# A fused attention, MoE and MLP kernel: landing times in the attention planner, four one-hot tiles on ScalarE, the experts' order chain in PSUM

## The chip, the cores and the metric

One core of a Trainium2 chip runs the whole program in one launch. The metric is the device time of that launch in microseconds, the median of several runs. The profile is one more execution of the same program, taken by the hardware profiler.

## The reference, cut to what matters

```
x = attention(q, k, v, omega)     # 4 x 8 heads x 576 x 64, random features, 128 of them
x = x.reshape(2304, 512)
logits = x @ w_gate               # 8 experts
e = argmax(logits); gate = softmax(logits)[e]
x[mask_e] = gate * (relu(x[mask_e] @ w1[e]) @ w2[e])     # 512 -> 1024 -> 512
h = x @ w_in                      # 512 -> 2048
g = where(h >= 1, h, where(h <= -1, 0, (h + 1)**2 / 4))
out = g @ w_out                   # 2048 -> 512
```

Attention here is linear: `phi(x) = exp(x @ omega.T - |x|^2 / 2 - max)`, then `phi(q) @ (phi(k).T @ v)`, divided by `phi(q) @ sum(phi(k))`.

## The kernel before, in words

Three stages follow each other: attention with routing, the experts, and the last MLP.

**Attention.** The 2304 tokens are 18 tiles of 128. Keys and queries are loaded in blocks and worked on in 36 units of half a block. A unit is: four transposes on TensorE (L646), a copy to SBUF on ScalarE (`th`, L651), 16 projections onto omega, each issued for both halves (L658), the row maximum on VectorE (L663), the bias (L670), and eight exponentials on ScalarE in two sets of four (`pp`, L674). The squares of a block are taken on ScalarE for keys (`sqt`, L600) and on GpSimd for queries, and are summed on GpSimd and VectorE into `nsq`. Key units end in the products with v (L699) and a copy `kvz` (L703); query units in transposes, a product with `kvz` and a copy `nx` (L774) for each tile.

**Routing** works on two tiles at a time (`r_tasks`): argmax, counts, and for each tile a one-hot row over 384 places, `ob` (L918, `one_b`), from which TensorE builds the list of tokens of each expert (`place`, L926). For the last pair of tiles this ends in `gidx` (L935), the list of the first expert's tokens. The last two tiles also scale their rows (L878 on ScalarE, L881 on VectorE) and store them to `xd` (L889, L892).

**What sets the order.** The attention stage is not issued in the order of the code. Every step is handed to `Plan.add` with an engine, a cost in ns, a rank, the steps that it follows and the buffers that it takes. A table of numbers, `NUDGES`, shifts the ranks. `Plan.run` then plays the stage with these costs and writes the instructions out in the order of the starts that it found. On the chip each engine runs its own list in that order and waits on semaphores. Costs are therefore no times: they only decide the order.

**The order chain** (L1080 to L1122) is some 40 small VectorE instructions between attention and the experts. It sorts the experts by their number of tokens, and moves the lists accordingly. It reads the counts `pn`, which lie in a PSUM tile of the attention's ring (`ps0`).

**The start of the experts** (`m_x0`, from L1202). GpSimd gathers the first expert's tokens from `xd` in three pieces (L1177). TensorE in the meantime runs 14 warm-up multiplications of ones (L1209) into a PSUM tile `idle`, then transposes the first piece (L1183), 3 more warm-ups, the second piece, 3 more, and the third. ScalarE splits the result (`xh`, L1189), and the first real multiplication is L1230:

```
idle = ps_h.tile([P, 512], F32, name="ph", tag="ph").rearrange("p (a f) -> p a f", a=4)
for i, _ in rows(0):
    for _ in range((14, 3, 3)[i]):
        nc.tensor.matmul(idle, lhsT=oneb, rhs=oneb.rearrange("p (o f) -> p o f", o=1).to_broadcast([P, 4, P]),
                         start=True, stop=True)
    for d in range(4):
        m_turn(0, d, i, px[d])
```

The pool of `idle` (`ps_h`) is opened after that of the attention's ring (`psp`) is closed, in the same eight PSUM banks; a tile of it is written only when the tile that lay there has been read for the last time.

Of the kernel before, what the change touches and what calls it, by code (L numbers as in the profile page):

```python
# [19 lines left out]
P = 128  # L20
# [65 lines left out]
class Plan:  # L86
# [7 lines left out]
    SLACK = 10.0  # L94
    HOPS = {"PE": {"PE": 30.0, "ACT": 200.0, "DVE": 200.0, "POOL": 200.0, "SP": 200.0},
# [26 lines left out]
    def run(self):  # L122
# [8 lines left out]
        at = {t[0]: 0.0 for t in self.tasks}  # L131
# [80 lines left out]
def kernel(  # L212
# [268 lines left out]
    with ExitStack() as actx:  # L481
# [59 lines left out]
        def omega_tasks():  # L541
# [12 lines left out]
            def scaled():  # L554
                nc.scalar.activation(oms, at(pb)[:, 0, :], AF.Copy, scale=SCALE)

            def tri():
                nc.vector.tensor_copy(trib, cs[:, C_TRI:C_TRI + P])

            x = add("SP", 1300, load_cs, 0)  # L560
            add("DVE", 130, tri, 8, after=[x])
            x = add("SP", 100, load, -7.5)
            x = add("PE", 110, turn, -5, after=[x], take=[pb], mode="whole")
            return add("ACT", 240, scaled, -5, after=[x], use=[pb])

        wgr = ac.tile([P, 4, E], F32, name="wgr")
# [509 lines left out]
        def flat(t):  # L1076
            return t[:, :, 0]
# [679 lines left out]
```

## Time and profile before

| | |
|---|---|
| three runs | 775.65, 777.16, 778.07 us; median 777.16 |
| the profiled execution | 776.65 us, of which its span is 774.9 |
| TensorE busy | 745.1 us, 96% of the span |
| VectorE, ScalarE, GpSimd busy | 515.7, 436.7, 376.6 us |
| mean granted TensorE clock | 0.991 of full speed |

Busy time is the time in which an engine had an instruction in flight, so a TensorE at 96% is not one at its peak; what an engine waits for is read from the stage concerned. Times in the rows below are microseconds from the start of the span, unless marked ns.

### The profile page before, as it was taken

What the parts mean: (1) busy time and instruction counts of PE and PEld (TensorE: products, weight loads), DVE (VectorE), ACT (ScalarE), POOL (GpSimd) and SP (SyncE); (2) the same over time, 40 slices, a digit from 0 to 9 for tenths busy, and PEclk for the clock granted to TensorE, in tenths of its full rate; (3) what the DMA queues carried; (4) which work ended last, traced back from release to release, by engine and by line L of the source; (5) the groups of instructions that cost most, each with busy time, mean ns of one, the idle gap of its engine ahead of it and who ended that gap; (6) DMA issues with size and microseconds to landing.
All of it is one profiled execution on the core that took longest, in us unless ns stands there. A gap on an engine that the chain in (4) does not pass through costs nothing. (4 is left out here: it accounts for less than half of the span.)

```text
span 774.9 us, 17116 instructions
## 1 busy us (share of the span) xinstructions
PE 745.1 (96%) x6476; PEld 684.0 (88%) x6476; DVE 515.7 (67%) x1104; ACT 436.7 (56%) x1061; POOL 376.6 (49%) x429
## 2 busy tenths in 40 slices
PE   5799999699999999999999999899999999999997
PEld 4698899489999999999988889788998899889985
DVE  3688888965667567565686775876656766575553
ACT  5999999353322222222477766676577655763441
POOL 6665951645654564425548875323343143343212
PEclk9999999899999999999999999999999999999999
DMA  9949511356765765655537769798696996977822
GB/s 231 230 100 255 158 69 30 123 166 179 213 193 178 221 212 179 207 166 161 163 117 305 274 249 330 285 328 269 177 375 189 307 319 168 332 239 285 315 97 85
DMA packets 94236, 164.25 MB, mean 212 GB/s; under 512 B 28528, under 2 KB 61424, under 8 KB 94144
## 3 DMA queue, kind: packets, MB, share of 16 engines
q1 hardware_dynamic: 79680, 94.96, 39.2%
q0 software_dynamic: 14112, 67.44, 27.0%
q8 instruction: 53, 0.87, 0.4%
q10 hardware_dynamic: 352, 0.66, 0.3%
q14 instruction: 39, 0.32, 0.1%
HBM read 122.93 MB, written 40.11 MB: 210 GB/s over the span
## 5 line engine op out<-in xcount | busy, mean ns | idle before, releaser
L1433 PE MATMUL po<-wh,g 128*128 128x512 f32 x288 | 113.8, 395 | 0.7 <-ACT st L1439 0.7
L1435 PE MATMUL po<-wh,g 128*128 128x512 f32 x288 | 113.9, 395 | 0.0
L1434 PE MATMUL po<-wl,g 128*128 128x512 f32 x288 | 113.6, 395 | 0.0
L351 POOL TENSOR_TENSOR wl<-wz,wh 128x256 fp32r<-128x256 f32 (+1 forms) x43 | 40.5, 948 | 95.3 <-ACT wh L365 92.8
L674 ACT ACTIVATE pp<-ps,bi 128x128 f32<-128x128 f32 x288 | 84.4, 487 | 0.0
L329 POOL TENSOR_SCALAR wh<-wra 128x1024 fp32r<-128x1024 f32 x43 | 50.2, 1170 | 61.2 <-DMA wra<-in_moe_w_dram 26.9
L1248 PE MATMUL py<-hh,wh 128*128 128x288 f32 (+6 forms) x256 | 77.5, 303 | 0.0
L1230 PE MATMUL ph<-xh,wh 128*128 128x288 f32 (+6 forms) x256 | 76.7, 300 | 0.7 <-ACT xh L1189 0.4
L1231 PE MATMUL ph<-xl,wh 128*128 128x288 f32 (+6 forms) x256 | 76.6, 299 | 0.1
L1250 PE MATMUL py<-hh,wl 128*128 128x288 f32 (+6 forms) x256 | 76.6, 299 | 0.0
L1232 PE MATMUL ph<-xh,wl 128*128 128x288 f32 (+6 forms) x256 | 76.5, 299 | 0.0
L1249 PE MATMUL py<-hl,wh 128*128 128x288 f32 (+6 forms) x256 | 76.3, 298 | 0.0
L1395 DVE TENSOR_TENSOR g<-cl,g 128x384 fp32r<-128x384 f32 x78 | 47.0, 603 | 38.9 <-ACT g L1391 37.9
L1235 ACT ACTIVATE hh<-ph 128x288 fp32r<-128x288 f32 (+6 forms) x64 | 26.7, 418 | 70.2 <-PE ph L1232 69.1
L1435 PEld LDWEIGHTS po<-wh,g 128*128 128x128 f32 x288 | 54.2, 188 | 13.1 <-DVE g L1395 0.4
L1433 PEld LDWEIGHTS po<-wh,g 128*128 128x128 f32 x288 | 54.2, 188 | 12.4 <-ACT st L1439 1.0
L1434 PEld LDWEIGHTS po<-wl,g 128*128 128x128 f32 x288 | 54.2, 188 | 11.5
L1236 DVE SCALAR_TENSOR_TENSOR hl<-ph,hh 128x288 fp32r<-128x288 f32 (+6 forms) x64 | 29.3, 461 | 52.0 <-ACT hh L1235 51.7
L1391 ACT ACTIVATE g<-cl 128x384 fp32r<-128x384 f32 x78 | 40.5, 520 | 39.7 <-DVE cl L1390 38.4
L441 DVE TENSOR_TENSOR wl<-wra,wh 128x1024 fp32r<-128x1024 f32 x43 | 61.0, 1421 | 2.4 <-POOL wh L329 2.4
L1253 ACT ACTIVATE yT<-py 128x288 f32<-128x288 f32 (+7 forms) x32 | 13.4, 418 | 83.6 <-PE py L1250 80.5
L663 DVE TENSOR_REDUCE nsq<-ps 128x4 f32<-128x512 f32 x72 | 48.1, 683 | 8.1 <-PE ps L658 8.0
(226 smaller groups left out, 2149.8 us busy)
## 6 DMA issues: line engine op xcount, KB each, us to landing
yS<-yd POOLq DMA_DIRECT2D x32, 768.0 KB, 12.2
wra<-in_moe_w_dram SPq DMA_DIRECT2D x43, 512.0 KB, 4.1
ys<-yd POOLq DMA_DIRECT2D x25, 768.0 KB, 11.9
wraw<-in_moe_w_dram SPq DMA_DIRECT2D x20, 512.0 KB, 4.0
yd<-tt SPq DMA_DIRECT2D x24, 384.0 KB, 2.7
yd<-ys SPq DMA_DIRECT2D x9, 768.0 KB, 4.3
wra<-in_moe_w_in_dram SPq DMA_DIRECT2D x12, 512.0 KB, 5.4
wra<-in_moe_w_out_dram SPq DMA_DIRECT2D x11, 512.0 KB, 7.6
```

Of the source, the lines that this page charges most:

```text
L329: nc.gpsimd.tensor_scalar(out=hi, in0=t, scalar1=1.0, scalar2=1.0, op0=ALU.mult, op1=ALU.mult)
L441: nc.vector.tensor_sub(lo, t, hi.bitcast(F32))
L674: act.activation(at(ppb)[:, 2 * j + i, :], at(pjb[i])[:, j, :], AF.Exp, bias=r["bi"][:, j, i:i + 1])
L1230: nc.tensor.matmul(ph, lhsT=wh[:, d, c], rhs=xh, start=(d == 0), stop=False)
L1231: nc.tensor.matmul(ph, lhsT=wh[:, d, c], rhs=xl, start=False, stop=False)
L1232: nc.tensor.matmul(ph, lhsT=wl[:, d, c], rhs=xh, start=False, stop=(d == 3))
L1248: nc.tensor.matmul(py, lhsT=wh[:, a, c], rhs=hh, start=(f == 0), stop=False)
L1249: nc.tensor.matmul(py, lhsT=wh[:, a, c], rhs=hl, start=False, stop=False)
L1250: nc.tensor.matmul(py, lhsT=wl[:, a, c], rhs=hh, start=False, stop=(f == 7))
L1433: nc.tensor.matmul(po, lhsT=gh[:, c], rhs=wh, start=(f == 0), stop=False)
L1434: nc.tensor.matmul(po, lhsT=gh[:, c], rhs=wl, start=False, stop=False)
L1435: nc.tensor.matmul(po, lhsT=gl[:, c], rhs=wh, start=False, stop=(f == 3))
```

## The change

Three things, in one diff.

1. The planner: the loads' costs are changed (a block 2250 to 1900 ns, a v 6500 to 6000, a weight 1460 to 1900, and others), the loading queue starts at 1150 ns instead of 0 (`FIRST`), and the table `NUDGES` of 1,058 numbers is another one.
2. Four tiles' one-hot rows (`OBA`, tiles 12, 13, 14 and 16) are made on ScalarE, in two instructions for each: the square of place number minus own place (`away`), and relu(1 - square). VectorE makes the negated places for them (`nr`).
3. The order chain keeps `key`, `at_`, `hot` and `offe` in the PSUM tile `ps0`, where the counts lie, and copies of two of them in SBUF, so that most of its two-input instructions read one input from PSUM and one from SBUF.

```
@@ -38,... @@ NUDGES
-    2, -4, -40, -16, 43, -44, 37, -6, 17, -2, -26, 9, -18, 36, -44, -2, -29, -37, 32, -32, -8, -18, 33, 26, -23,
+    -15, -7, -43, -28, -21, -43, -16, -42, 35, -34, -15, -42, 3, 5, -16, -22, 37, 25, -34, -44, -10, -35, 16, -44,
...
     SLACK = 10.0
+
+    FIRST = {"SP": 1150.0}
...
-        at = {t[0]: 0.0 for t in self.tasks}
+        at = {t[0]: self.FIRST.get(t[0], 0.0) for t in self.tasks}
...
-            x = add("SP", 1300, load_cs, 0)
+            x = add("SP", 900, load_cs, 0)
...
-            x = add("SP", 100, load, -7.5)
+            x = add("SP", 500, load, -7.5)
...
-            o["load"] = add("SP", 1800 if small else 2250, load, rank - 8, take=[o["buf"]])
+            o["load"] = add("SP", 1900, load, rank - 8, take=[o["buf"]])
...
             def mine2():
+                if any(t0 + j in OBA for j in range(n)):
+                    r["nr"] = ap.tile([P, n], F32, name="nr", tag="nr", bufs=3)
+                    dve.reduce_sum(r["nr"], r["pr"], axis=AX, negate=True)
                 dve.reduce_sum(rk, r["pr"], axis=AX)
...
                 r["ob", j] = ap.tile([P, NB * P], BF16, name="ob", tag="ob", bufs=4)
+                if t0 + j in OBA:
+                    away = ap.tile([P, NB * P], F32, name="away", tag="away", bufs=1)
+                    act.activation(away, cs[:, C_IOTA:C_IOTA + NB * P], AF.Square, bias=r["nr"][:, j:j + 1])
+                    act.activation(r["ob", j], away, AF.Relu, scale=-1.0, bias=1.0)
+                    return
...
-                ws.append(add("DVE", 430, lambda j=j: one_b(j), rank + 0.4, after=[x, places[-1]], use=[pb]))
+                ws.append(add(*(("ACT", 880) if t0 + j in OBA else ("DVE", 475)), lambda j=j: one_b(j), rank + 0.4,
+                              after=[x, places[-1]], use=[pb]))
...
+        OBA = (12,13,14,16)
...
-        n, key, at_, nums, off, offe = [small(f"t{i}", [P, E, 1]) for i in range(6)]
+        pn = plan.tiles["ps"][0]
+        sums, key, at_ = [pn[:, 0, 16 * i:16 * i + E] for i in range(3)]
+        hot = pn[:, 1, 0:E * E].rearrange("p (a b) -> p a b", a=E)
+        nums, off, n, keys = [small(f"t{i}", [P, E, 1]) for i in range(4)]
+        offe = pn[:, 3, 0:E].rearrange("p (e o) -> p e o", o=1)
...
-        pn = plan.tiles["ps"][0][:, 0, :]
-        nc.tensor.matmul(pn[:, 0:E], lhsT=oneb, rhs=rsb[:, NTILE, :], start=True, stop=True)
-        dve.memset(ones, 1.0)
-        dve.tensor_copy(flat(n), pn[:, 0:E])
-        dve.scalar_tensor_tensor(out=flat(key), in0=flat(n), scalar=8.0, in1=col(C_C8, E), op0=ALU.mult, op1=ALU.add)
-        dve.memset(key[:, 0, :], 0.0)
-        dve.tensor_tensor(out=prod[:, 0], in0=row(key), in1=key.to_broadcast([P, E, E]), op=ALU.is_lt)
+        nc.tensor.matmul(sums, lhsT=oneb, rhs=rsb[:, NTILE, :], start=True, stop=True)
+        dve.scalar_tensor_tensor(out=key, in0=sums, scalar=8.0, in1=col(C_C8, E), op0=ALU.mult, op1=ALU.add)
+        dve.tensor_scalar(out=key[:, 0:1], in0=key[:, 0:1], scalar1=0.0, scalar2=None, op0=ALU.mult)
+        dve.tensor_copy(flat(keys), key)
+        dve.tensor_copy(flat(n), sums)
+        dve.tensor_tensor(out=prod[:, 0], in0=line(key), in1=keys.to_broadcast([P, E, E]), op=ALU.is_lt)
...
         dve.reduce_sum(flat(offe), prod[:, 0], axis=AX)
...
         nc.vector.tensor_tensor(out=rr, in0=ohall, in1=offe.rearrange("p e o -> p o e").to_broadcast([P, NTILE, E]), op=ALU.mult)
```

In the changed kernel all lines after the new ones are numbered higher, by 2 in the units, by 10 in the routing's end, and by 19 from the order chain's end on: L646 is now L648, L658 is L660, L674 is L676, L1183 is L1202, L1209 is L1228, L1230 is L1249.

**Where the order moves: the start of attention, on TensorE.** The rows are the first of TensorE's list; of the projections of a unit the first stands for all 16. Before:

```order
L646 MATMUL ps_134<-ident,blk_142 128x128 x4
L552 MATMUL ps_135<-ident,om_205 128x128
L646 MATMUL ps_136<-ident,blk_143 128x128 x4
L658 MATMUL ps_137<-oms,th_151 64x128
...
L658 MATMUL ps_139<-oms,th_152 64x128
...
L646 MATMUL ps_141<-ident,blk_144 128x128 x4
```

Now:

```order
L648 MATMUL ps_134<-ident,blk_142 128x128 x4
L554 MATMUL ps_135<-ident,om_205 128x128
L660 MATMUL ps_136<-oms,th_151 64x128
...
L648 MATMUL ps_138<-ident,blk_143 128x128 x4
L648 MATMUL ps_139<-ident,blk_144 128x128 x4
L660 MATMUL ps_140<-oms,th_152 64x128
```

The first unit's projections (`th_151`) stood behind the transposes of the second block (`blk_143`) and directly ahead of the second unit's (`th_152`), with the third block's transposes (`blk_144`) behind both; now they come first, and both blocks' transposes stand together ahead of the second unit's projections.

**The end of attention, on ScalarE.** The rows follow the last copy of a tile's result (`nx`); `rex` are the softmax's exponentials, `blk` with 128x64 the scaled rows of a last tile. Before:

```order
L861 ACTIVATE rex<-ps_138 128x16
L858 ACTIVATE rex,rga<-lall,rmx 128x8 x2
L878 ACTIVATE blk_142<-nx_174,dall 128x64 x4
L889 DMA xd<-blk_148 64x512
L1189 ACTIVATE xh<-px 128x288 x2
```

Now:

```order
L863 ACTIVATE rex<-ps_136 128x16
L925 ACTIVATE away<-cs,nr 128x384
L926 ACTIVATE ob<-away 128x384
L925 ACTIVATE away<-cs,nr 128x384
L926 ACTIVATE ob<-away 128x384
L860 ACTIVATE rex,rga<-lall,rmx 128x8 x2
L880 ACTIVATE blk_143<-nx_171,dall 128x64 x4
L925 ACTIVATE away<-cs,nr 128x384
L926 ACTIVATE ob<-away 128x384
L891 DMA xd<-blk_146 64x512
L925 ACTIVATE away<-cs,nr 128x384
L926 ACTIVATE ob<-away 128x384
```

Two pairs of `away` and `ob` (tiles 12 and 13) now stand between the exponentials of the tiles before and those of the last two, a third pair behind the scaled rows, and the fourth behind the store that ScalarE issues.

**The order chain, on VectorE.** The rows begin at `gidx`, the first expert's list; `ps_134` is the tile `ps0`, in which the counts lie, `hot`, `t` and `trr` are the chain's own tiles. Before:

```order
L935 TENSOR_TENSOR gidx<-slots,ps_136 128x3
L936 TENSOR_TENSOR slots<-slots,ps_136 128x24
L1081 MEMSET u_3063 128x8
L1082 COPY t_3056<-ps_134 128x8
L1083 SCALAR_TENSOR_TENSOR t_3057<-t_3056,cs 128x8
...
L1103 TENSOR_TENSOR prod<-hot,t_3060 128x64
L1104 TENSOR_REDUCE t_3061<-prod 128x8
...
L1115 TENSOR_TENSOR trr<-seen,t_3061 128x144
L1116 TENSOR_REDUCE tsp<-trr 128x18
```

Now:

```order
L945 TENSOR_TENSOR gidx<-slots,ps_139 128x3
L946 TENSOR_TENSOR slots<-slots,ps_139 128x24
L1099 SCALAR_TENSOR_TENSOR ps_134<-ps_134,cs 128x8
L1100 TENSOR_SCALAR ps_134<-ps_134 128x1
L1101 COPY t_3073<-ps_134 128x8
...
L1121 TENSOR_TENSOR prod<-ps_134,t_3071 128x64
L1123 TENSOR_REDUCE ps_134<-prod 128x8
...
L1134 TENSOR_TENSOR trr<-seen,ps_134 128x144
L1135 TENSOR_REDUCE tsp<-trr 128x18
```

The last instruction that reads `ps_134` was the copy at L1082, the second of the chain; it is now the product `trr` at L1134, near its end.

## Rows read from the trace of the kernel before

**Rows 1.** The page, part 1: each engine's busy time, share and instructions.
```profile
PE 745.1 (96%) x6476; PEld 684.0 (88%) x6476; DVE 515.7 (67%) x1104; ACT 436.7 (56%) x1061; POOL 376.6 (49%) x429
```

**Rows 2.** Windows by stage: length, busy us of five engines, granted clock, DMA.
```profile
5.40:15.00 9.60, 8.01 (x96) 6.77 (x97) 3.33 (x10) 5.04 (x8) 6.19 (x7) 1.00 1.10 290
...
15.00:38.00 23.00, 18.08 (x412) 15.09 (x404) 16.16 (x46) 21.82 (x75) 15.83 (x16) 0.93 1.08 225
...
38.00:138.00 100.00, 99.11 (x2222) 89.18 (x2219) 84.68 (x325) 98.09 (x322) 60.04 (x78) 1.00 0.47 121
...
142.80:151.00 8.20, 2.19 (x41) 1.57 (x40) 7.63 (x41) 1.83 (x10) 4.83 (x10) 0.77 0.46 160
...
170.00:774.90 604.90, 595.30 (x3487) 553.32 (x3485) 386.67 (x603) 298.36 (x624) 273.39 (x280) 1.00 0.69 229
```

**Rows 3.** ScalarE's timeline at the start: start, us, line, tiles, idle before.
```profile
7.20 0.27 ACT L555 ACTIVATE oms<-ps 128x128 f32<-128x128 f32 x1
...
8.12 0.63 ACT L600 ACTIVATE sqt<-blk 128x512 f32<-128x512 f32 x1 [0.65 <-DMA blk<-in_k_dram]
...
9.78 1.05 ACT L600 ACTIVATE sqt<-blk 128x1024 f32<-128x1024 f32 x1
...
13.95 1.16 ACT L651 ACTIVATE th<-ps 128x512 f32<-128x512 f32 x2 [3.13 <-PE ps L646]
...
15.01 3.19 ACT L674 ACTIVATE pp<-ps,bi 128x128 f32<-128x128 f32 x12
```

**Rows 4.** TensorE's and VectorE's timelines at the start.
```profile
9.18 3.69 PE L658 MATMUL ps<-oms,th 64*64 64x128 f32 x64
...
12.80 1.68 PE L646 MATMUL ps<-ident,blk 128*128 128x128 f32 x8
...
11.22 0.69 DVE L663 TENSOR_REDUCE nsq<-ps 128x4 f32<-128x512 f32 x1 [1.88 <-PE ps L658]
```

**Rows 5.** ScalarE's waits from 5 to 38.3 us: in total, times, longest.
```profile
ACT kvz L703 <- PE ps L699: 1.2, 1, 1.2
```

**Rows 6.** VectorE's timeline at the end of attention and in the order chain.
```profile
142.85 0.18 DVE L781 TENSOR_REDUCE dall<-nx 128x8 f32<-128x16 f32 x1
...
149.27 1.02 DVE L918 TENSOR_TENSOR ob<-cs,ps 128x384 bf16<-128x384 f32 x2
...
150.81 0.16 DVE L935 TENSOR_TENSOR gidx<-slots,ps 128x3 uint32<-128x3 f32 x1 [0.43 <-PE ps L1080]
...
151.11 0.15 DVE L1082 COPY t<-ps 128x8 f32<-128x8 f32 x1
...
156.41 0.30 DVE L1115 TENSOR_TENSOR trr<-seen,t 128x144 f32<-128x144 bf16 x1
```

**Rows 7.** ScalarE's timeline at the end of attention.
```profile
142.40 0.41 ACT L774 ACTIVATE nx<-ps 128x292 f32<-128x292 f32 x1 [0.70 <-PE ps L771]
...
144.42 0.30 ACT L858 ACTIVATE rex<-lall,rmx 128x8 f32<-128x8 f32 x1 [1.53 <-DVE rmx L836]
...
146.75 0.82 ACT L878 ACTIVATE blk<-nx,dall 128x64 f32<-128x64 f32 x3 [1.65 <-issue]
```

**Rows 8.** Groups of ScalarE's instructions by line, from 385 us on.
```profile
L1383 ACT ACTIVATE cl<-cl 128x384 f32<-128x384 f32 x77 | 40.5, 526 | 2.4
```

**Rows 9.** TensorE's timeline and its waits at the experts' start.
```profile
151.32 4.50 PE L1209 MATMUL ph<-oneb 128*128 128x512 bf16 x14 [0.53 <-DVE t L1082]
...
155.69 0.41 PE L1183 MATMUL px<-ident,xg 128*128 128x128 f32 x2
...
159.13 0.40 PE L1230 MATMUL ph<-xh,wh 128*128 128x288 f32 x1 [0.44 <-ACT xh L1189]
...
PEld px L1183 <- DMA xg<-xd,gidx: 0.6, 1, 0.6
```

**Rows 10.** Windows in the warm-up multiplications (after the busy times the granted clock).
```profile
153.50:154.00 0.50, 0.50 (x3) 0.22 (x2) 0.47 (x5) 0.00 (x0) 0.50 (x1) 0.50 0.44 82
...
154.00:154.50 0.50, 0.50 (x4) 0.20 (x3) 0.50 (x6) 0.00 (x0) 0.38 (x1) 1.00 0.65 180
```

More of the change, by code (lines that the diff above doesn't have):

```diff
@@ L1016 @@
             if s == 1:
-                vload[0] = add("SP", 6500, lambda: load_v(0), s - 1)
+                vload[0] = add("SP", 6000, lambda: load_v(0), s - 1)
                 x = add("SP", 50, gate_weights, s)
@@ L1020 @@
             if s == 5:
-                vload[1] = add("SP", 6500, lambda: load_v(1), s - 5)
+                vload[1] = add("SP", 6000, lambda: load_v(1), s - 5)
             done[u] = unit_tasks(u, blocks[which, blk], s, prev)
@@ L1028 @@
                 if hf == 1 and b + 2 < B:
-                    vload[b + 2] = add("SP", 6500, lambda b=b: load_v(b + 2), s + 3, after=[last_head])
+                    vload[b + 2] = add("SP", 6000, lambda b=b: load_v(b + 2), s + 3, after=[last_head])
             new = []
@@ L1045 @@
                 wb = buf("wra")
-                x = add("SP", 1460, lambda key=key, wb=wb: w_load(key, at(wb)), s - 2, take=[wb])
+                x = add("SP", 1900, lambda key=key, wb=wb: w_load(key, at(wb)), s - 2, take=[wb])
                 x = add("POOL", 1050, lambda key=key: w_split(key), s + 1, after=[x], use=[wb])
@@ L1052 @@
                 wb = buf("wra")
-                add("SP", 1460, lambda key=key, wb=wb: w_load(key, at(wb)), s - 2, take=[wb])
+                add("SP", 1900, lambda key=key, wb=wb: w_load(key, at(wb)), s - 2, take=[wb])
         assert wk == 6
@@ L1065, in col @@
             return cs[:, c:c + n]
-        n, key, at_, nums, off, offe = [small(f"t{i}", [P, E, 1]) for i in range(6)]
+        pn = plan.tiles["ps"][0]
[3 more added lines that the diff above has]
+        offe = pn[:, 3, 0:E].rearrange("p (e o) -> p e o", o=1)
         inc, ones, nv = [small(f"u{i}", [P, E]) for i in range(3)]
-        hot, prod = small("hot", [P, E, E]), small("prod", [P, NB, E, E])
+        prod = small("prod", [P, NB, E, E])
@@ L1070, with column, line @@
         g = prod[:, 0:2].rearrange("p m a b -> p (m a b)").rearrange("p (e j) -> p e j", j=16)
         tot = small("ttot", [P, 1])
-        def row(t):
-            return t.rearrange("p a o -> p o a").to_broadcast([P, E, E])
+        def column(t):
+            return t.rearrange("p (e o) -> p e o", o=1).to_broadcast([P, E, E])
+        def line(t):
+            return t.rearrange("p (o e) -> p o e", o=1).to_broadcast([P, E, E])
         def flat(t):
             return t[:, :, 0]
-        pn = plan.tiles["ps"][0][:, 0, :]
@@ L1080 @@
-        nc.tensor.matmul(pn[:, 0:E], lhsT=oneb, rhs=rsb[:, NTILE, :], start=True, stop=True)
-        dve.memset(ones, 1.0)
-        dve.tensor_copy(flat(n), pn[:, 0:E])
-        dve.scalar_tensor_tensor(out=flat(key), in0=flat(n), scalar=8.0, in1=col(C_C8, E), op0=ALU.mult, op1=ALU.add)
-        dve.memset(key[:, 0, :], 0.0)
-        dve.tensor_tensor(out=prod[:, 0], in0=row(key), in1=key.to_broadcast([P, E, E]), op=ALU.is_lt)
-        dve.reduce_sum(flat(at_), prod[:, 0], axis=AX)
-        iota = col(C_IOTA, E).rearrange("p (e o) -> p e o", o=1)
@@ L1088 @@
-        dve.tensor_tensor(out=hot, in0=iota.to_broadcast([P, E, E]), in1=row(at_), op=ALU.is_equal)
-        dve.tensor_tensor(out=prod[:, 0], in0=hot, in1=row(n), op=ALU.mult)
-        dve.tensor_tensor(out=prod[:, 1], in0=hot, in1=row(iota), op=ALU.mult)
+        nc.tensor.matmul(sums, lhsT=oneb, rhs=rsb[:, NTILE, :], start=True, stop=True)
+        dve.scalar_tensor_tensor(out=key, in0=sums, scalar=8.0, in1=col(C_C8, E), op0=ALU.mult, op1=ALU.add)
+        dve.tensor_scalar(out=key[:, 0:1], in0=key[:, 0:1], scalar1=0.0, scalar2=None, op0=ALU.mult)
@@ new lines @@
+        dve.tensor_copy(flat(keys), key)
+        dve.tensor_copy(flat(n), sums)
+        dve.tensor_tensor(out=prod[:, 0], in0=line(key), in1=keys.to_broadcast([P, E, E]), op=ALU.is_lt)
+        dve.reduce_sum(at_, prod[:, 0], axis=AX)
+        dve.tensor_tensor(out=hot, in0=column(col(C_IOTA, E)), in1=line(at_), op=ALU.is_equal)
+        dve.tensor_tensor(out=prod[:, 0], in0=hot, in1=line(flat(n)), op=ALU.mult)
+        dve.tensor_tensor(out=prod[:, 1], in0=hot, in1=line(col(C_IOTA, E)), op=ALU.mult)
@@ L1093 @@
         dve.tensor_copy(ints[:, 4, :], inc)
+        dve.memset(ones, 1.0)
         dve.tensor_tensor_scan(out=inc, data0=ones, data1=flat(nums), initial=0.0, op0=ALU.mult, op1=ALU.add)
@@ L1102 @@
         dve.tensor_copy(gidx[:, :, 1:E], slots[:, :, 1:E])
-        dve.tensor_tensor(out=prod[:, 0], in0=hot.rearrange("p r e -> p e r"), in1=row(off), op=ALU.mult)
+        dve.tensor_tensor(out=prod[:, 0], in0=hot.rearrange("p r e -> p e r"), in1=line(flat(off)),
+                          op=ALU.mult)
         dve.reduce_sum(flat(offe), prod[:, 0], axis=AX)
```

82 rows, old and new, of the table NUDGES are left out of this document.

## The prediction

> **What bounds the kernel now.** I read the page's busy shares first [rows 1], then windows by stage, since a share over the whole span says nothing about a stage. Of the span, 604.9 us lie behind 170 us, and there TensorE is busy for 595.3 [rows 2]. All three edits lie ahead of that, so what matters is when the experts' first real multiplication starts, at 159.13 us [rows 9]; from there on TensorE is the bound, has no slack worth naming, and passes every microsecond on to the end. In attention, from 38 to 138 us, ScalarE is busy for 98.09 and TensorE for 99.11 of 100 us [rows 2]. ScalarE is what I count by: its list is mostly exponentials, its work is the same in any order, and only 1.9 us of idle time are left there for a better order to find. At the start there is more: from 5.4 to 15 us ScalarE works 5.04 of 9.6 us, and from 15 to 38 us 21.82 of 23. Between attention and experts, 142.8 to 151 us, ScalarE works 1.83 of 8.2 us and VectorE 7.63: there VectorE is the bound. The last stretch, 150.97 to 159.13, is the gather, the warm-ups and the transposes [rows 6, 9].
>
> **The planner.** What the new order does at the start is followed on TensorE and ScalarE. Before, TensorE ran the projections of two units in one piece of 3.69 us from 9.18, and only then the next transposes, at 12.80; ScalarE, done with the third square (9.78 and 1.05 us), waited 3.13 us for them and began its exponentials at 15.01 [rows 3, 4]. Now the first unit's projections come alone. `th_151` stands behind the 0.27 us of `oms`, so is ready near 7.7; half of 3.69 us brings TensorE to 9.6; two blocks' transposes, 1.68 us as in the row at 12.80, to 11.3 [rows 3, 4]. ScalarE squares the second block from 8.12 to 8.75, waits for its transposes until about 10.6, copies (0.6), squares (1.05) and copies the third block, and is free at 12.8. VectorE needs two maxima of 0.69 us after 9.6 [rows 4] and the biases, so is done by 11.5. The exponentials thus begin at 12.8 rather than 15.01, with one copy of 0.6 us (half of 1.16) still to do: 1.6 us gained. Further on, the 1.18 us that ScalarE waited for the first v products [rows 5] go, since those now stand ahead of two units' projections in TensorE's list while ScalarE still has finished maxima to work on. I take back 0.3 for a bias that then waits on a late square. Sum: **-2.5 us**. Bounds: nothing, if the lead is lost again, and -5.7, if all idle time of ScalarE from 5.4 to 38 us went (4.56 and 1.18).
>
> In the middle, 38 to 138 us, I take **0**: the order is new, but no row says that it waits more or less. Bounds: -1.9, all of ScalarE's idle time there, and +2.4, two new waits like the one of 1.18 us.
>
> **The four one-hot rows.** On VectorE one costs 0.47 us, by the next instruction's start (two take 1.02 us in all [rows 6]); four of them less two reductions for `nr` and one added sum are -1.6 us of VectorE's 8.12 us between the last copy's sum (142.85) and the end of `gidx` (150.97). On ScalarE no row shows this pair. The nearest is a square in place over the same 128x384, 0.526 us [rows 8]; I take that for both instructions, 1.05 us for a tile. They don't lie in idle time for free, because ScalarE's list is in order: from the last copy of `nx` (142.81) follow the small exponentials (0.2), tiles 12 and 13 (2.1), the exponentials of the last two tiles (two of 0.30 with their sums read, 0.7, which before began at 144.42 and now find ScalarE busy), the gate and its reciprocal on VectorE (0.6), the scaled rows (0.82 for three, 1.1 for four [rows 7]), tile 14 (1.05), the store (0.4), tile 16 (1.05), then TensorE's placing and VectorE's sum (0.7: from 149.27 to 150.97 less the two one-hot rows' 1.02 [rows 6]); 0.2, 0.6 and 0.4 are estimates from the gaps between the rows. That makes 7.9 us, against 8.16 before: ScalarE takes over from VectorE as what ends last, and little is left, **-0.2 us**. Bounds: -1.9, if VectorE alone decides (four times 0.47), and +1.2, if ScalarE is held by the store and both reciprocals.
>
> **The order chain.** Its own length hardly changes: a memset becomes a dependent operation and a copy comes in, +0.15 us by steps of 0.2 as at 151.11; instructions with PSUM on one side take as long as those with SBUF alone. What changes is who waits for it. The first warm-up starts at 151.32 and was released by VectorE's copy L1082, the last reader of the counts' bank [rows 9, 6]. In the change that bank is read until the product `trr`, the old L1115, which ends at 156.71 [rows 6]. So TensorE stands still through the whole chain: from the end of `gidx` to the first warm-up it was 0.35 us, and will be 5.74 (150.97 to 156.71) + 0.15 + 0.06 = 5.95, **+5.6 us**. Behind it are queued all 14 warm-ups (4.50 us), the three groups of transposes, ScalarE's split and L1230. From the first warm-up to L1230 it was 7.81 us [rows 9]. The gathers, which took part in that (the weight load waited 0.6 us for one [rows 9]), are long landed then: **-0.3**, bounds 0 and -0.6. GpSimd, the gathers and VectorE don't wait for TensorE there, but nothing on the path waits for them either, so what they may gain is not seen.
>
> **The sum**: -2.5 + 0 - 0.2 + 5.6 - 0.3 = +2.6 us. The profiled execution took 776.65 us, 0.5 below the median of 777.16; 776.65 + 2.6 = **779.3 us**, 0.34% above the profiled execution. A difference of 0.3%, 2.3 us, is about what a measurement of this kernel can tell from no change, so the forecast is a slower kernel by just that much.
>
> **The rivals.**
>
> *The lead is lost in the middle.* The start gains 2.5 us, but in-order lists on four engines near full give it back: a block or a buffer that comes 2.5 us late for a ScalarE that is early. For it: VectorE too is busy for 84.68 of the 100 us [rows 2]. Against it: the lists hold the same work. 781.8 us, 0.20.
>
> *The clock stays low.* Up to 154 us the granted clock is 0.5, the lower of the two levels (1.2 GHz), and it rises 2.7 us after the first warm-up [rows 9, 10]; TensorE had done only small pieces since 142.8, at a mean of 0.77 [rows 2]. In the change it stands wholly still for 5 us before. If all 14 run at the lower level, the 1.7 us that they ran at the upper one take twice as long, +1.7: 781.0 us, 0.07. The Trainium skill ("TensorE: Matmul & The Clock Gate", "Part 1: The HAM clock gate") says that an idle array falls to the lower level, comes back only after sustained work, and that the number of matmuls at the lower level differs from run to run; by its 426.7 ns for one of 512 columns there, 14 would be an estimated 6.0 us instead of 4.50. The trace has the fall and the rise, in one execution, and cannot show the spread.
>
> *No change that can be measured.* The middle finds the 1.9 us as well: 777.4 us, 0.12. Here the planner's gain pays for the late warm-ups.
>
> *Faster: the warm-ups don't wait.* It hangs on one place, the PSUM tile of the warm-ups. If it lay in another bank than the counts, or were released by something earlier than `trr`, the +5.3 us fall away and 776.65 - 2.7 = 774.0 us are left. For it: a matmul's wait can name several engines, and the profile picks one. Against it: the 0.53 us of idle time before 151.32 end with the copy's end at 151.26, to 0.06 us [rows 6, 9]. It decides when TensorE starts its warm-ups less than 0.7 us after `gidx`. 0.06.
>
> **How the numbers follow.** The forecast has 0.55; its own range is 777.8 to 780.8, and 779.0, the bound of slower by 0.3% from the profiled execution, lies in it, so I give 0.30 of it to slower and 0.25 to no difference. Slower: 0.30 + 0.20 + 0.07 = 0.57. Same: 0.25 + 0.12 = 0.37. Faster: 0.06. The range has to reach the lost lead and the paid-for case: its top is the 781.8 of the one with 0.7 for the tail, 782.5; its bottom is the 777.4 of the other less another 1.4 of the start's bound, 776.0. The bounds of all terms together, 772 to 787, would need everything on one side.
>
> **What would show it.** Right: the first warm-up starts about 6 us after `gidx` ends, released by `trr`; TensorE idle ahead of it; L1249 comes 13.5 us after `gidx` instead of 8.16; the first exponentials near 13 us; the last `nx` copy 2 to 3 us before 142.4; `gidx` about 8 us behind that. Wrong: warm-ups within 1 us of `gidx`; a ScalarE in the middle with more than 4 us of waits, or an attention that ends more than 6 us earlier.

## The result, and the profile after

| | before | after |
|---|---|---|
| median, measured side by side | 776.51 us (774.76 to 778.07) | 782.84 us (780.63 to 784.38) |
| ratio, 95% interval | | 1.0066 (1.0047 to 1.0086) |
| profiled execution, its span | 776.65, 774.9 | 782.84, 781.0 |

The change made the kernel slower by 0.66%, twice the 0.34% that was forecast; the median lies 0.3 us above the top of the range, and the ratio on the profiled execution's own 776.65 us gives 781.8, which lies in it. In the two profiled executions the spans differ by 6.1 us. Five marks cut them into stages (all are starts of an instruction, in us):

| mark | before | after | the stage up to it |
|---|---|---|---|
| first exponentials, `pp` | 15.01 | 12.71 | -2.30 |
| last exponentials | 135.74 | 135.67 | 120.73 to 122.96, +2.23 |
| `gidx` | 150.81 | 150.86 | 15.07 to 15.19, +0.12 |
| first expert product, `ph` from `xh` | 159.13 | 164.45 | 8.32 to 13.59, +5.27 |
| end of the span | 774.9 | 781.0 | 615.77 to 616.55, +0.78 |

The rows come from the timelines of the changed kernel: start, duration, engine, line, tiles, and in brackets the idle time before and what ended it. They answer to [rows 3, 6, 9].

```profile
12.71 1.14 ACT L676 ACTIVATE pp<-ps,bi 128x128 f32<-128x128 f32 x4
...
14.01 2.37 DVE L577 COPY wgb<-wgr 64x32 f32<-64x32 f32 x2
...
13.76 0.74 POOL L609 TENSOR_TENSOR sqt<-sqt 128x256 f32<-128x256 f32 x1
14.44 1.91 POOL L604 TENSOR_TENSOR sqt<-blk 128x1024 f32<-128x1024 f32 x1
...
17.34 1.14 ACT L676 ACTIVATE pp<-ps,bi 128x128 f32<-128x128 f32 x4 [1.75 <-DVE bi L672]
...
135.67 1.31 ACT L676 ACTIVATE pp<-ps,bi 128x128 f32<-128x128 f32 x4
...
150.86 0.16 DVE L945 TENSOR_TENSOR gidx<-slots,ps 128x3 uint32<-128x3 f32 x1 [0.91 <-PE ps L1098]
...
156.64 0.29 DVE L1134 TENSOR_TENSOR trr<-seen,ps 128x144 f32<-128x144 bf16 x1
...
156.99 4.56 PE L1228 MATMUL ph<-oneb 128*128 128x512 bf16 x14 [6.14 <-DVE trr L1134]
...
164.45 0.40 PE L1249 MATMUL ph<-xh,wh 128*128 128x288 f32 x1 [0.36 <-ACT xh L1208]
```

The last three rows are the forecast's main term as it was put: TensorE stands still for 6.14 us, `trr` ends at 156.93, the warm-ups start 0.06 us later. The first rows hold what the forecast missed. ScalarE begins at 12.71, and 4.6 us later it waits 1.75 us for the biases `bi`, which VectorE computes. VectorE at that time makes two copies of 64x32, `wgb`, which take 2.37 us; in the kernel before the same two took 0.35, at 24.95. The two lines are the copies one by one in the changed kernel (durations in ns, shortest, median and longest, and the starts), and the pair in the kernel before:

```profile
L577 DVE COPY wgb<-wgr x2: 518/1180/1841, 14.0 to 14.5; 64x32 f32<-64x32 f32 x2
...
24.95 0.35 DVE L575 COPY wgb<-wgr 64x32 f32<-64x32 f32 x2
```

The first ends at 14.53 and the second at 16.38, each 0.03 us after an instruction of GpSimd (14.50 and 16.35).

Of the windows by stage, three follow on this wait (length, busy time of PE, PE's weight loads, DVE, ACT and POOL with counts, granted clock, DMA share, GB/s), and two answer to [rows 2].

```profile
15.00:20.00 5.00, 2.84 (x72) 2.31 (x64) 4.90 (x13) 3.25 (x12) 3.73 (x4) 0.99 1.22 269
20.00:25.00 5.00, 4.41 (x47) 3.16 (x40) 3.04 (x10) 5.00 (x16) 3.01 (x3) 0.50 0.99 227
25.00:30.00 5.00, 4.74 (x75) 3.44 (x73) 4.93 (x10) 4.15 (x15) 4.01 (x2) 0.83 1.10 227
...
38.00:138.00 100.00, 98.03 (x2204) 88.84 (x2200) 80.02 (x321) 97.49 (x323) 59.86 (x78) 1.00 0.46 119
142.80:151.00 8.20, 1.99 (x41) 1.55 (x41) 6.93 (x45) 6.34 (x18) 5.24 (x12) 0.70 0.48 160
```

From 15 to 20 us ScalarE works for 3.25 of 5 us and TensorE, which waits for it, for 2.84; from 20 to 25 TensorE's granted clock is the lower of its two levels (0.50, 1.2 GHz), and ScalarE loses another 0.85 us from 25 to 30. In the middle ScalarE is as full as before (97.49 to 98.09 of 100 us), so in this profile the lead is gone by 38 us, not lost bit by bit.

### The profile page after: what moved, and what is told of

Its sections match the earlier page's. It is cut to its first block, busy times and chain, and to the rows that moved or that the text cites. A ratio compares the mean times of both kernels' runs of the same rounds, so it can differ in the third digit from the quotient of the medians.

```text
span 781.0 us, 17138 instructions
## 1 busy us (share of the span) xinstructions
PE 745.9 (96%) x6476; PEld 684.8 (88%) x6476; DVE 515.6 (66%) x1104; ACT 440.4 (56%) x1069; POOL 379.8 (49%) x429
## 3 DMA queue, kind: packets, MB, share of 16 engines
q1 hardware_dynamic: 79680, 94.96, 38.3%
## 5 line engine op out<-in xcount | busy, mean ns | idle before, releaser
L676 ACT ACTIVATE pp<-ps,bi 128x128 f32<-128x128 f32 x288 | 85.5, 488 | 2.0 <-DVE bi L672 2.0
L1249 PE MATMUL ph<-xh,wh 128*128 128x288 f32 (+6 forms) x256 | 76.6, 299 | 0.6 <-ACT xh L1208 0.4
L1454 PEld LDWEIGHTS po<-wh,g 128*128 128x128 f32 x288 | 54.2, 188 | 13.1 <-DVE g L1414 0.4
```

Source lines behind the costliest of these rows:

```text
L676: act.activation(at(ppb)[:, 2 * j + i, :], at(pjb[i])[:, j, :], AF.Exp, bias=r["bi"][:, j, i:i + 1])
L1249: nc.tensor.matmul(ph, lhsT=wh[:, d, c], rhs=xh, start=(d == 0), stop=False)
L1454: nc.tensor.matmul(po, lhsT=gl[:, c], rhs=wh, start=False, stop=(f == 3))
```

## The experiments

The theory behind them: the chain's hold on PSUM costs the 5.3 us; the planner's lead is real, and is lost because plain copies from SBUF to SBUF on VectorE are held while GpSimd is in an instruction. The rival: the new orders themselves are slower. Twelve kernels were run; each row has the ratio to the kernel before on the same chip, and the marks of one profiled execution.

| kernel | median (range, runs), us | ratio, 95% | first exponentials | last | `gidx` | first expert product | span |
|---|---|---|---|---|---|---|---|
| old chain | 773.78 (772.75 to 778.98, 12) | 0.9957 (0.9938 to 0.9976) | 12.40 | 131.56 | 146.74 | 155.54 | 772.3 |
| chain alone | 783.67 (782.45 to 786.50, 6) | 1.0066 (1.0049 to 1.0083) | 13.34 | 137.56 | 152.62 | 167.82 | 784.6 |
| planner alone | 777.76 (776.82 to 780.10, 12) | 1.0001 (0.9988 to 1.0013) | 12.73 | 135.66 | 151.92 | 160.57 | 776.9 |
| rows alone | 776.43 (774.03 to 781.32, 12) | 0.9978 (0.9957 to 1.0000) | 12.65 | 133.97 | 148.32 | 157.69 | 775.3 |
| short hold | 777.63 (775.91 to 779.22, 12) | 0.9995 (0.9982 to 1.0008) | 13.34 | 133.40 | 148.59 | 159.16 | 776.8 |
| warm-ups in the ring | 777.85 (774.81 to 781.89, 12) | 0.9995 (0.9978 to 1.0012) | 12.65 | 139.36 | 154.56 | 163.80 | 780.0 |
| maxima | 781.30 (779.95 to 784.76, 8) | 1.0051 (1.0033 to 1.0069) | 12.63 | 132.81 | 148.01 | 162.31 | 778.9 |
| old chain, maxima | 774.94 (773.29 to 776.21, 7) | 0.9963 (0.9947 to 0.9979) | 12.51 | 133.06 | 148.25 | 157.15 | 773.1 |
| planner alone, maxima | 777.76 (776.74 to 778.95, 12) | 1.0001 (0.9989 to 1.0013) | 13.32 | 133.80 | 150.06 | 158.72 | 775.0 |
| six copies | 778.29 (776.62 to 780.85, 12) | 1.0006 (0.9988 to 1.0024) | 12.28 | 136.93 | 152.12 | 160.79 | 777.0 |
| six maxima | 774.57 (773.46 to 776.18, 12) | 0.9959 (0.9946 to 0.9973) | 12.51 | 134.33 | 149.52 | 158.10 | 773.9 |
| no copies | 773.67 (773.24 to 775.30, 7) | 0.9953 (0.9936 to 0.9970) | 12.42 | 132.66 | 147.85 | 156.39 | 771.8 |

### The order chain: four kernels

**Old chain**: the changed kernel with the third part of the change taken back.

```diff
-        pn = plan.tiles["ps"][0]
-        sums, key, at_ = [pn[:, 0, 16 * i:16 * i + E] for i in range(3)]
...
+        n, key, at_, nums, off, offe = [small(f"t{i}", [P, E, 1]) for i in range(6)]
...
```

> The changed kernel with the order chain of before put back; planner's start and the four one-hot rows stay. Theory (the chain's results in PSUM keep TensorE from its warm-ups, and nothing else of the change costs anything): the first warm-up comes within 0.5 us of gidx again, L1230 and its followers 5.3 us earlier against gidx than in the changed kernel, and the time falls from 782.8 to about 777.5, which is not to be told from before. Rival (the new orders of work are what slows, and the late warm-ups are paid back before the experts begin): the warm-ups come early, but the time stays near 782.

**Chain alone**: the kernel before with that part and nothing else.

> The kernel before with the new order chain and nothing else. Theory: the first warm-up waits for trr and comes 6 us after gidx, and the time rises by the 5.3 us found between the two traces, from 776.5 to about 781.8. Rival (the new orders slow): no change from before, 776.5.

**Short hold**: the changed kernel, whose chain reads PSUM for the last time early.

```diff
-        hot = pn[:, 1, 0:E * E].rearrange("p (a b) -> p a b", a=E)
+        hot = small("hot", [P, E, E])
...
-        offe = pn[:, 3, 0:E].rearrange("p (e o) -> p e o", o=1)
+        offe = small("t4", [P, E, 1])
```

> The changed kernel with hot and offe in SBUF: the chain's last reader of PSUM is then the comparison that makes hot, four operations behind key, and no longer the one that makes trr. Theory (TensorE's warm-ups wait for the last reader of the attention's PSUM, whichever tile it reads): the first warm-up comes about 1.6 us after gidx in place of 6, L1230 some 4 us sooner, and the time is about 778.7, 4.1 less than the changed kernel. Rival (the wait is for trr itself, or the warm-ups' place doesn't matter): the first warm-up stays 6 us behind gidx, or it comes early and the time stays near 782.

**Warm-ups in the ring**: the hold stays, the warm-ups go elsewhere.

```diff
+        warm = plan.tiles["ps"][4]
+        for _ in range(14):
+            nc.tensor.matmul(warm, lhsT=oneb, rhs=oneb.rearrange("p (o f) -> p o f", o=1).to_broadcast([P, 4, P]),
+                             start=True, stop=True)
...
-                for _ in range((14, 3, 3)[i]):
+                for _ in range((0, 3, 3)[i]):
```

> The changed kernel with its first 14 warm-up products written into a free tile of attention's PSUM ring, right behind the sums product, in place of the experts' own PSUM. Theory: the warm-ups begin within 0.5 us of gidx although the chain still holds its PSUM; the transposes of the first gathered rows still wait for trr, at about 157, and the 4.4 us that the warm-ups took behind trr are gone: L1230 at about 160.0 against gidx at 151.0, time about 778.4. Rival (what costs is that the clock is low when the experts begin, not the place in the queue): the products behind trr run at the low clock again and 2 us or more of the 4.4 come back, 780.5 or above.

TensorE's timelines, first of the old chain, then of the chain alone, the short hold and the ring:

```profile
147.26 5.39 PE L1221 MATMUL ph<-oneb 128*128 128x512 bf16 x14 [0.53 <-DVE t L1094]
155.54 0.40 PE L1242 MATMUL ph<-xh,wh 128*128 128x288 f32 x1 [0.36 <-ACT xh L1201]
```

```profile
158.71 6.13 PE L1216 MATMUL ph<-oneb 128*128 128x512 bf16 x14 [6.10 <-DVE trr L1122]
167.82 0.40 PE L1237 MATMUL ph<-xh,wh 128*128 128x288 f32 x1 [0.44 <-ACT xh L1196]
```

```profile
150.29 5.98 PE L1228 MATMUL ph<-oneb 128*128 128x512 bf16 x14 [1.71 <-DVE hot L1105]
159.16 0.40 PE L1249 MATMUL ph<-xh,wh 128*128 128x288 f32 x1 [0.36 <-ACT xh L1208]
```

```profile
154.41 5.59 PE L1101 MATMUL ps<-oneb 128*128 128x512 bf16 x14
160.72 0.41 PE L1206 MATMUL px<-ident,xg 128*128 128x128 f32 x2 [0.72 <-DVE trr L1138]
163.80 0.40 PE L1253 MATMUL ph<-xh,wh 128*128 128x288 f32 x1 [0.37 <-ACT xh L1212]
```

The releaser in the brackets moves with the chain's last reader of PSUM (`t`, `hot`, `trr`), and TensorE's standstill with it: 0.53, 1.71, 6.10 us. From `gidx` to the first expert product it is 8.3 to 9.4 us in the nine profiles with the old chain, 10.6 with the short hold, 9.2 with the warm-ups in the ring, and 13.6, 14.3 and 15.2 in the three with the chain as changed. So it is the warm-ups' place behind the hold that costs. In time the short hold and the ring both came to 0.9995 of before, 5.5 us under the changed kernel's 1.0066, where 4.1 and 4.4 us had been expected; the rivals had 780.5 or more. The 15.2 of the chain alone is more than the standstill: there the 14 warm-ups also took 6.13 us, against 4.50 in the kernel before. The ring also shows that the experts' first transposes wait for `trr` in the same way, but only 0.72 us, since the warm-ups have run by then.

The chain alone costs 0.66%, 5.1 us, which is by itself as much as the whole change (1.0066 both). The old chain however did not give the 777.5 that the theory had, but 773.8: in its profile the hold is gone and `gidx` comes 4.1 us earlier besides. The first half of the theory stands, "nothing else costs anything" fell. What the rest was is the next question.

### The lead at the start: seven kernels

**Planner alone**: the old chain, and all one-hot rows on VectorE (`OBA = ()`).

> The changed kernel with the order chain of before and all one-hot rows on VectorE: of the change only the planner's landing times are left. Theory: the first exponentials come at 12.7 again, the wgb copies take about 2.4 us and ScalarE waits some 1.7 us for bi near 17 us, TensorE's clock falls between 20 and 25 us, and so attention's end and the whole stand within 1 us of before, 776 to 777.5. Rival (the early start holds without the rest of the change): 774.5, the prediction's own 2.5 us less.

**Maxima**: the changed kernel with the `wgb` copies in a form that is no plain copy. **Old chain, maxima** has both mends, **planner alone, maxima** has this one on the kernel above.

```diff
-                nc.vector.tensor_copy(wgb[64 * i:64 * i + 64, :, 8 * i:8 * i + 8], wgr[64 * i:64 * i + 64])
+                nc.vector.reduce_max(wgb[64 * i:64 * i + 64, :, 8 * i:8 * i + 8],
+                                     wgr[64 * i:64 * i + 64].rearrange("p c (e o) -> p c e o", o=1), axis=AX)
```

> The changed kernel with the two wgb copies on VectorE written as a maximum over an axis of length one; same elements, no plain copy from SBUF to SBUF. Theory (a plain copy from SBUF to SBUF is held off while GpSimd works): the two take 0.2 to 0.4 us each in place of 2.37 in all, ScalarE's wait of 1.75 us for bi near 17 us is gone, TensorE's clock doesn't fall between 20 and 25 us, attention's end comes 1 to 2 us sooner, and the time is 781 to 782. Rival (they wait for their load, or the lead is lost to other waits in the middle): the copies take as long, or the wait goes and attention ends where it did, 782.8.

> Both mends at once: the changed kernel with the old order chain and with the wgb copies as a maximum. Theory: the two gains add, 782.8 less 5.3 less 1 to 2, so 775.5 to 776.5, at or just below before. Rival (the lead at the start is lost in any case): 777.5, as with the old chain alone.

> The planner's landing times alone (old order chain, all one-hot rows on VectorE), with the two wgb copies as a maximum over an axis of length one. With plain copies this kernel took 777.8, the same as before, while its profile shows the copies held for 2.34 us. Theory (each plain copy is held until GpSimd's instruction in flight ends, and a held start costs 2.5 to 4 us by the end of attention): no run starts held, and the time falls 2 to 3 us below, to about 775, ratio 0.996 to 0.998. Rival (the planner's start brings nothing; what was gained with it came from the one-hot rows on ScalarE): 777.8 again, ratio 1.000.

**Six copies** and **six maxima**: the old chain, and `for _ in range(3):` around the copies, in the one form and the other.

> The changed kernel with the old order chain and each of the two wgb copies made three times, six plain copies in a row, 1.05 us at the 0.17 us that one takes alone. With two copies nine of twelve runs took 773 to 774.5 and three 777 to 779. Theory: six don't fit between two instructions of GpSimd, so some are held in every run, the six take over 2 us, and all runs lie at 776.5 to 779. Rival (the two groups of times come from something else): both groups stay, with the median within 1 us of 773.8.

> The control to the six copies: the same six written as a maximum over an axis of length one. Theory: none is held, the six take about 1.05 us in all, and the time is at most 0.7 us above the 774.9 of the two maxima. Rival (any 0.7 us more on VectorE at this place brings the late start): it goes to 777 or above, like the six copies.

**No copies**: old chain, the maxima, and the cast to `trib` as a maximum too.

```diff
-                nc.vector.tensor_copy(trib, cs[:, C_TRI:C_TRI + P])
+                nc.vector.reduce_max(trib, cs[:, C_TRI:C_TRI + P].rearrange("p (f o) -> p f o", o=1), axis=AX)
```

> The old chain with the wgb copies as a maximum, and VectorE's cast that makes trib as a maximum too: no plain copy between SBUF tiles is left at attention's start. With the cast as a cast it took 0.22 to 1.93 us in the profiles so far, and 0.42 us in this kernel's nearest kin. Theory: it takes 0.2 us in any execution, the runs lie close together at 773 to 775, and the kernel is 3 us below before. Rival (the cast never was in the way): the same as with the cast, 774.9, spread included.

The timelines of the six copies: VectorE, GpSimd, ScalarE.

```profile
13.75 4.41 DVE L578 COPY wgb<-wgr 64x32 f32<-64x32 f32 x6
...
11.98 2.09 POOL L610 TENSOR_TENSOR sqt<-sqt 128x512 f32<-128x512 f32 x2 [2.52 <-ACT sqt L603]
14.03 1.89 POOL L605 TENSOR_TENSOR sqt<-blk 128x1024 f32<-128x1024 f32 x1
16.00 2.12 POOL L610 TENSOR_TENSOR sqt<-sqt 128x512 f32<-128x512 f32 x2
...
19.11 1.14 ACT L677 ACTIVATE pp<-ps,bi 128x128 f32<-128x128 f32 x4 [3.54 <-DVE bi L673]
```

And of the six maxima:

```profile
13.79 1.22 DVE L578 TENSOR_REDUCE wgb<-wgr 64x32 f32<-64x32 f32 x6
...
14.25 1.89 POOL L606 TENSOR_TENSOR sqt<-blk 128x1024 f32<-128x1024 f32 x1
...
15.96 1.14 ACT L678 ACTIVATE pp<-ps,bi 128x128 f32<-128x128 f32 x4 [0.59 <-DVE bi L674]
```

Same data, same place, same work of GpSimd beside it: six copies take 4.41 us and end at 18.16, as GpSimd's additions do at 18.12; six maxima take 1.22 us, 0.20 each, straight through it. ScalarE waits 3.54 us in the one and 0.59 in the other, and the medians are 778.29 and 774.57. This shows the hold by itself, and a price of 3.7 us for these six copies (1.0006 and 0.9959, with intervals that don't meet). The six copies' twelve runs all lie at 776.6 or above, as expected, four of them above the 779 foreseen; the six maxima stay within their bound. The Trainium skill ("SBUF — State Buffer", "Who interferes with whom") says that copies and casts on VectorE can enter a mode that takes a port pair shared with GpSimd, and that who comes second is blocked for the whole instruction; these rows agree, to 0.04 us. The maxima over an axis of length one were not held in any profile here.

Two copies are held in some profiles only. In the old chain's they found a gap:

```profile
13.27 0.35 DVE L577 COPY wgb<-wgr 64x32 f32<-64x32 f32 x2
...
12.11 1.27 POOL L609 TENSOR_TENSOR sqt<-sqt 128x512 f32<-128x512 f32 x1 [2.53 <-ACT sqt L602]
13.46 0.77 POOL L609 TENSOR_TENSOR sqt<-sqt 128x256 f32<-128x256 f32 x1
```

The first ends about when GpSimd's addition ends (13.38), and the second starts before the next begins (13.46). In the changed kernel the copies came 0.74 us later, at 14.01, and fell into the additions. From the first exponentials to the last it takes 119.2 to 120.6 us in the six profiles of the planner's order without a held copy (six maxima, with 0.86 us more work, not counted), and 122.9, 123.0, 124.7 and 126.7 in the four with one. By these profiles the hold cost the changed kernel 2.7 us (122.96 less 120.24, the profile of no copies); the 126.7 has other waits in the middle too.

A middle can be long without a held copy, however. The chain alone, in the order of before, took 124.2 us from the first exponentials to the last, against 120.7 before, and its copies took 0.37 us. ScalarE worked 94.81 of the 100 us from 38 to 138, where it worked 98.09 before; its two longest waits there, and the window:

```profile
ACT qt L758 <- PE ps L754: 1.7, 1, 1.7
ACT pp L674 <- DVE bi L670: 1.1, 1, 1.1
...
38.00:138.00 100.00, 97.50 (x2188) 87.72 (x2187) 83.83 (x315) 94.81 (x312) 58.38 (x76) 0.98 0.46 120
```

So one profile's middle doesn't give the hold's price; the pair of six copies and six maxima does, for six. With the new chain, the medians show less of it: 1.0051 with the maxima in place of 1.0066, and the intervals overlap. In the maxima's own profile both take 0.36 us, inside and across GpSimd's additions, ScalarE's wait for `bi` is gone, and `gidx` comes 2.85 us sooner than in the changed kernel, more than the 1 to 2 us expected:

```profile
13.28 0.36 DVE L577 TENSOR_REDUCE wgb<-wgr 64x32 f32<-64x32 f32 x2
```

The old chain with the maxima took 774.94, below the 775.5 to 776.5 expected, and can't be told from the old chain with its copies (0.9963 and 0.9957). No copies came out as its theory had it, 773.2 to 775.3 and 3.7 us below before, but its 0.9953 can't be told from the 0.9963 with the cast either, so its rival is not excluded.

The planner alone, with the maxima, was the theory's miss: 777.8 in place of 775. Its rival was met to the digit (777.8, 1.000): what had been gained with the planner came only together with the one-hot rows on ScalarE. Its middle is as short as in the others without a held copy (120.48 us), and still nothing is gained over before. The rows show one reason: the stage behind it is longer.

### The one-hot rows: one kernel, and the marks of all

**Rows alone**: the kernel before with `OBA = (12,13,14,16)` and the pair of activations for these tiles.

> The kernel before with the four one-hot rows on ScalarE and nothing else. Theory: the stretch from VectorE's last dall sum to gidx is 0.2 to 0.4 us shorter than before's 8.12, and the time 776.1 to 776.3, which can't be told from before. Rival (the pair of activations holds TensorE's place product back, 1.79 us of wait seen once in the changed kernel, and gidx comes later): gidx 0.5 to 1 us later, 777 to 777.5.

From the last exponentials to `gidx` the time is the same within 0.02 us for each order of the work and each place of the rows:

| | rows on VectorE | rows on ScalarE |
|---|---|---|
| order of before | 15.07, 15.06 | 14.35 |
| order of the changed planner | 16.26, 16.26 | 15.19, 15.18, 15.19, 15.20, 15.20, 15.19, 15.19, 15.19, 15.19 |

VectorE's timeline of planner alone, behind the last exponentials on ScalarE:

```profile
135.66 1.31 ACT L676 ACTIVATE pp<-ps,bi 128x128 f32<-128x128 f32 x4
...
149.16 1.48 DVE L928 TENSOR_TENSOR ob<-cs,ps 128x384 bf16<-128x384 f32 x3
150.70 0.18 DVE L948 TENSOR_TENSOR slots<-slots,ps 128x24 f32<-128x24 f32 x1
150.80 0.55 DVE L928 TENSOR_TENSOR ob<-cs,ps 128x384 bf16<-128x384 f32 x1
151.92 0.16 DVE L945 TENSOR_TENSOR gidx<-slots,ps 128x3 uint32<-128x3 f32 x1 [0.58 <-PE ps L1092]
```

The planner's new order puts four one-hot rows at the very end of VectorE's list, where before the last two stood ([rows 6], 149.27). It lengthens the end of attention by 1.19 us, and the rows on ScalarE take 1.07 of it back. Neither the theory nor the rival had this: the rival about TensorE's wait for `ob` did not come (`gidx` is earlier), and the expected 0.2 to 0.4 us were 0.72 (0.74 from the last `dall` sum, as the expectation counts). By the ratios the rows on ScalarE bring more than this stage shows: 1.7 us alone, with an interval that reaches 1.0000, and 3.4 and 3.0 with the planner (old chain against planner alone, without and with the maxima). Where the rest comes from is not shown.

## Why the prediction was right in direction and half in size

**The order chain and the gathers, +5.6 and -0.3: right.** +5.27 was measured in the pair, 5.1 alone; from the first warm-up to the first expert product 7.81 us became 7.46, as the -0.3 has it. The reason given, the wait for `trr`, is shown by the dose: three last readers, three lengths of standstill.

**The clock of the warm-ups** (the rival at 781.0): not what happened here, 14 took 4.56 us after and 4.50 before. But over the profiles they took 4.49 to 6.13 us, the spread that the Trainium skill's rule ("TensorE: Matmul & The Clock Gate", "Part 1: The HAM clock gate") led to and one trace couldn't show; 6.13, in the chain alone, is close to the 6.2 of the rival. The standstill ahead doesn't decide it: 4.56 came behind 6.14 us of it, and 5.98 behind the short hold's 1.71.

**The tail, -0.2: two things of opposite sign.** -0.72 for the rows on the order of before, or -1.07 on the new one, and +1.19 from the planner's new order, which the prediction read only at the start of attention. Measured +0.12 together, from the last exponentials on. In the prediction's own stretch, from the end of the last `nx` copy to the end of `gidx`, 8.16 us became 8.03, where its sum had 7.9.

**The planner's start, -2.5: the step that failed.** The chain of events was right: first exponentials at 12.71, predicted 12.8, and no wait for the first v products. But the sign that it gave for the end of attention failed: the last `nx` copy came at 142.58, not 2 to 3 us before 142.4. Two things were wrong. First, the 15.01 of before was one draw. In two more executions of the same order (chain alone, rows alone) the first exponentials began at 13.34 and 12.65, and the wait for v products was 0.8 us and none. The 3.69 us from 9.18 on which the sum rests [rows 4] were there (chain alone, then rows alone):

```profile
8.54 3.21 PE L658 MATMUL ps<-oms,th 64*64 64x128 f32 x64
```

```profile
8.12 2.94 PE L658 MATMUL ps<-oms,th 64*64 64x128 f32 x64
```

The planner's order has 12.28 to 13.34 in eleven profiles, with a median of 12.63; against the two that is a gain of 0 to 0.7 us. Second, "in the middle 0" was +2.23 in the pair of profiles; the held copies are the cause that the rows show for it, though the medians with the maxima don't confirm its size. The planner alone is at 1.0001: its start gains little, and its end gives that back.

**The rival that came true** is "the lead is lost in the middle", 781.8; 1.0066 times 776.65 is 781.8. That it agrees to the digit is luck: its lead of 2.5 us hardly existed, as the draw of 15.01 shows, and the chain alone reaches the same ratio. Its place was right (a late bias for an early ScalarE), its mechanism was not a full list but a held copy, and by 38 us it was over. The argument against it, "the lists hold the same work", fails because the same instruction has no fixed duration: the two copies took 0.35 us where they stood before and 2.37 where the planner put them.

**The sum again**, from the pair: -2.30 + 2.23 + 0.12 + 5.27 + 0.78 = 6.1. The last term, in the experts, has no cause that was found; from the first expert product to the end the twelve experiments' profiles took 615.4 to 617.6 us, so 0.78 is within their spread. In the prediction, the bounds of the single terms add up to 772.2 and 785.9; the 787 there is a slip.

**What is left open.** As far as the profiles show, a copy is held when it comes while GpSimd is in an addition. The old chain's twelve runs fall into nine at 772.8 to 774.4 and three at 777.3 to 779.0, and whether the three are held ones is open. For it: their mean granted clock is 0.985 to 0.988, where the nine have 0.992 to 0.994 and the six copies 0.985 to 0.990. Against it: the short hold's runs part in the same way, five at 775.9 to 776.3, one at 777.2 and six at 778.1 to 779.2, and its profile is one of the six (778.73) though its copies took 0.41 us in all. Only one of the old chain's twelve has a trace. That the copies' form changed nothing in the medians of planner alone (777.76 both times, though 2.34 us against 0.36 in the two profiles) isn't explained. And between the changed kernel and its old-chain twin lie 9 us of median, 8.5 by the ratios, where the chain explains 5.1 (alone) to 6.8 (with the maxima on both sides) and the hold 2.7 in a profile.

**The better version** is no copies: 0.9953 (0.9936 to 0.9970) of before, 3.7 us faster, and the closest set of runs; the old chain, old chain with maxima and six maxima lie within its interval. It keeps the planner and the rows and drops the new chain.

## What to carry to other kernels

When work is moved to PSUM to save operands, ask who waits for those banks: the last reader, not the first, sets when the next stage's first write may start. When a schedule moves a plain SBUF copy or cast on VectorE under GpSimd's work, its duration is no longer its own; the same copy written as a maximum took 0.2 us wherever it stood in these runs. And a start-up time read from one execution is a draw: 2.4 us lay between three executions of one order.

## What was not expected of the hardware

A copy of 64x32 took 0.17 us, or 0.52 and 1.84 in the changed kernel, the end set by GpSimd's instruction each time; the cast to `trib` took 0.22 to 1.93 us over the profiles, and 0.27 as a maximum.

TensorE's first products change speed while the granted clock reads 1.00 throughout: one projection of 64x128 takes 0.42 us at first and 0.27 later, and the step came between 12.7 and 13.1 us in the changed kernel, between 11.5 and 12.0 in the old chain. The second unit's projections, which the copies follow, are (changed kernel, then old chain):

```profile
11.54 1.80 PE L660 MATMUL ps<-oms,th 64*64 64x128 f32 x32
```

```profile
11.23 1.36 PE L660 MATMUL ps<-oms,th 64*64 64x128 f32 x32
```

Of the 0.74 us by which the copies came later in the changed kernel, some 0.44 are this difference in speed, and the rest is the later start. What sets the step itself no run shows.

The warm-ups' PSUM tile and the transposes' (`ph` and `px`) lie in different pools, and both waited for the last reader of the counts' one tile: the first with 6.14 us in the changed kernel, the second with 0.72 in the ring. This suggests that a closed pool is released as a whole; no run separates it from a wait of TensorE's that names the engine and not the tile.
